# Loading V tiles through GpSimd's DMA queue and K tiles and weights through SyncE's, in a decode kernel with a long key/value cache

## The chip, the cores and the metric

The kernel runs on one core of one Trainium2 chip, the other cores idle. The metric is the device time of one execution in microseconds (us), as the median of several executions. The profile's own span is about 2 us shorter than the device time (383.9 against 385.8 us for the kernel before).

## The reference, cut to what matters

One token is decoded through two branches, mixed by a sigmoid gate. Almost all of the work is the attention branch: 32 query heads share 4 key/value heads ("groups"), and the cache is 65,536 tokens long.

```python
B, Sq, D = (1, 1, 1024)
Hq, Hkv, Sk, Dh = (32, 4, 65536, 128)
...
q = (x @ wq)                                  # reshaped to 32 heads
scores = einsum('bhqd,bhkd->bhqk', q, k) * Dh ** (-0.5)
p = softmax(scores, axis=-1)
o = einsum('bhqk,bhkd->bhqd', p, v)           # k, v: each of 4 heads serves 8 query heads
a = o.reshape(B, Sq, Hq * Dh) @ wo
...                                           # b: a gated MLP with layer norm
return g * a + (1 - g) * b
```

K and V are 67.1 MB each in bfloat16, the weights another 27.8 MB. Each byte is used once, so this is a kernel of loads.

## The kernel before

Each group's K is read as four tiles of 4.19 MB (128 partitions of 32 KB), its V likewise. All large tiles rotate through one pool of four buffers, and one queue, SyncE's, issues every large load in program order:

```python
NKV = 4
kv = ctx.enter_context(tc.tile_pool(name="kv", bufs=NKV))
...
def load(src, shape, name):
    t = kv.tile([P, CT * P], BF16, name=name, tag="kv")
    ...                                        # v: a view of t in the wanted shape
    nc.sync.dma_start(out=v, in_=src)
    return v
```

The main loop works on K of group g beside V of group g-1, because V needs the softmax of the whole group:

```python
for g in range(G):
    for j in range(NT):                        # G = 4 groups, NT = 4 tiles
        k_tile(g, j, load_kv(A_k_cache, g, j, "kn"))
        if j == 1 and g + 1 < G:
            build_w(g + 1)
        if j == NT - 1:
            stats(g)                           # maximum, exp, transposes of the weights
        if g > 0:
            v_tile(g - 1, j, load_kv(A_v_cache, g - 1, j, "vt"))
        elif j == NT - 1:
            project(load(B_w_out..., "wout_t"), ...)
    if g > 0:
        head_out(g - 1)                        # evacuates V's sums, on DVE and PE
for j in range(NT):
    v_tile(G - 1, j, load_kv(A_v_cache, G - 1, j, "vt"))
head_out(G - 1)
...                                            # six loads of wo, 8.4 MB, and the last projection
```

`k_tile` transposes a K tile on DVE in four pieces (`kt`, line 320). When the fourth is done, the tile's buffer is free, and the K tile after the next may be loaded into it. `v_tile` multiplies on PE (line 372) and frees V's buffer. Since K and V loads alternate in program order, K holds two of the four buffers and V the other two.

The point to keep in mind is the order on DVE when a group ends: the maximum over the group, the transposed weights (`stats`), then `head_out(g-1)`, which needs PE to have finished group g-1's last V tile, and only then the transposes of the next group's first K tile.

Of the kernel before, what the change touches and what calls it, by code (L numbers as in the profile page):

```python
# [15 lines left out]
CT = 128  # L16
# [11 lines left out]
def kernel(  # L28
# [15 lines left out]
    nc = tc.nc  # L44

    _, _, D = A_x.shape
    _, G, S, DH = A_k_cache.shape
# [32 lines left out]
    def same_weights(ins):  # L80
        held.add(ins.ins.name)
# [14 lines left out]

    nc.at_finalize(drop_repeated_loads)

    def load(src, shape, name):
        t = kv.tile([P, CT * P], BF16, name=name, tag="kv")  # L100
        n = 1
        for s in shape:
            n *= s
        v = t[:, :n]
        if len(shape) == 2:
            v = v.rearrange("p (a b) -> p a b", b=shape[1])
        nc.sync.dma_start(out=v, in_=src)
        return v

    def load_kv(src, g, j, name):  # L110
        k0 = j * CT * P
        return load(src[0, g, k0:k0 + CT * P, :].rearrange("(p c) d -> p (c d)", c=CT),
                    (CT * DH,), name)


    xg8 = const.tile([KC, 2, P], BF16, name="xg8")
# [6 lines left out]
    KH = KC // 2  # L123
    win_view = B_w_in.rearrange("(p c) n -> p c n", c=KC)
    win_t = [load(win_view[:, i * KH:(i + 1) * KH, :], (KH, F), "win_t") for i in range(2)]
    wq_view = A_wq.rearrange("(p c) n -> p c n", c=KC)
    wq_t = [load(wq_view[:, i * KH:(i + 1) * KH, :], (KH, HD), "wq_t") for i in range(2)]


# [42 lines left out]
    for t in range(2):  # L172
        nc.vector.tensor_tensor(
            out=xm[:, t], in0=xb_ps[:, t * P:(t + 1) * P].rearrange("p (i c) -> p c i", c=KC),
# [51 lines left out]
    for hf in range(2):  # L226
        nc.vector.tensor_tensor(  # L227
            out=zm[:, hf], in0=z_ps[:, hf * HN:hf * HN + ZN].rearrange("p (j c) -> p j c", c=FC),
# [3 lines left out]
                            in_=zm.rearrange("p h j c -> p h c j"), axis=AX.X, op=ALU.add)  # L232
# [44 lines left out]
    for k in range(NHB):  # L277
        xs = slice(k * NX // NHB, (k + 1) * NX // NHB)
        nc.vector.tensor_tensor(  # L279
            out=qm[:, xs], in0=q_ps[:, k * HN:(k + 1) * HN].rearrange("p (x j e) -> p x j e",  # L280
                                                                   j=B, e=2),
# [6 lines left out]
        out=q4[:], in0=q1[:].rearrange("p x e -> p (x e)").unsqueeze(1).to_broadcast(  # L288
            [P, NB, NX * 2]),
# [7 lines left out]
    for g in range(G):  # L297
        k, t0 = g * T2 // NB, g * T2 % NB
        nc.vector.tensor_copy(out=qs[:, g].rearrange("p b (t h) -> p b t h", t=T2),
                              in_=qv[:, k, t0:t0 + T2].rearrange("p t h b -> p b t h"))  # L300

    def build_w(g):
        for v in range(VC):
            nc.vector.tensor_tensor(
                out=wt[g % 2][:, v, :, :, v, :],
                in0=qs[:, g].unsqueeze(2).to_broadcast([P, BP, NB, REP]),
                in1=own_n[:].unsqueeze(1).unsqueeze(3).to_broadcast([P, BP, NB, REP]),
                op=ALU.mult)
# [5 lines left out]
    def k_tile(g, j, kn):  # L314
        kb = kn.bitcast(I32)
        n = CC * DH // 2
        s_ps = pss.tile([P, 2 * HN], FP32, name="s_ps", tag="s")
        for v in range(VC):
            kt = ktp.tile([P, CC * DH], BF16, name="kt")
            nc.vector.transpose(out=kt[:].bitcast(I32), in_=kb[:, v * n:(v + 1) * n])  # L320
            while late:
                nc.vector.reduce_max(**late.pop())  # L322
            kx = kt[:].rearrange("p (c h k e) -> p h e c k", h=2, k=B, e=2)
            for b in range(BP):
                for k in range(2):
                    ins = nc.tensor.matmul(  # L326
                        s_ps[:, k * HN:(k + 1) * HN],
                        lhsT=wt[g % 2][:, v, b].rearrange("p a v h -> p (a v h)"),
                        rhs=kx[:, b // 2, b % 2, k * CC // 2:(k + 1) * CC // 2, :],
                        start=(v == 0 and b == 0), stop=(v == VC - 1 and b == BP - 1),  # L330
                        skip_group_check=True)
                    if k > 0:
                        same_weights(ins)
        if j == 0:
            mxs[g] = wk.tile([P, NT], FP32, name="mx")
        sct[g, j] = scp.tile([P, CC * B], BF16, name="sc")
        nc.scalar.copy(out=sct[g, j][:], in_=s_ps[:])  # L337
        late.append(dict(out=mxs[g][:, j:j + 1], in_=sct[g, j][:], axis=AX.X))

    def stats(g):  # L340
        nc.vector.reduce_max(**late.pop())  # L341
        m1 = wk.tile([P, 1], FP32, name="m1")
        nc.vector.reduce_max(out=m1[:], in_=mxs[g][:], axis=AX.X)  # L343
        mt_ps = psm.tile([1, P], FP32, name="mt_ps", tag="m")
        nc.tensor.transpose(mt_ps[:], m1[:], ident_f[:])  # L345
        gm = wk.tile([1, REP], FP32, name="gm")
        nc.vector.tensor_reduce(out=gm[:], in_=mt_ps[:].rearrange("p (a h) -> p h a", h=REP),
                                axis=AX.X, op=ALU.max)
        gr = wk.tile([1, P // REP, REP], FP32, name="gr")
        nc.vector.tensor_copy(out=gr[:], in_=gm[:].unsqueeze(1).to_broadcast([1, P // REP, REP]))  # L350
        nb_ps = psm.tile([P, 1], FP32, name="nb_ps", tag="m")
        nc.tensor.matmul(nb_ps[:], lhsT=gr[:].rearrange("p a h -> p (a h)"),  # L352
                         rhs=ones_f[0:1, 0:1], start=True, stop=True)
        nb = wk.tile([P, 1], FP32, name="nb")
        nc.vector.tensor_scalar(out=nb[:], in0=nb_ps[:], scalar1=-SCALE, scalar2=None,  # L355
                                op0=ALU.mult)
        lss[g] = wk.tile([P, NT], FP32, name="ls")
        for j in range(NT):
            nc.scalar.activation(out=sct[g, j][:], in_=sct[g, j][:], func=ACT.Exp, scale=SCALE,  # L359
                                 bias=nb[:, 0:1], accum_out=lss[g][:, j:j + 1])  # L360
            ptt[g, j] = ptp.tile([P, CC, B], BF16, name="pt")
            nc.vector.transpose(out=ptt[g, j][:].rearrange("p c x -> p (c x)"),  # L362
                                in_=sct[g, j][:])

    def v_tile(g, j, vt):
        if j == 0:
            o_ps[g] = pso.tile([P, 2, VC * DH], FP32, name="o_ps")
        vx = vt.rearrange("p (v c d) -> p c v d", v=VC, d=DH)
        for u in range(CC // 2):
            hs = slice(u % 2 * P // 2, (u % 2 + 1) * P // 2)  # L370
            for e in range(2):
                ins = nc.tensor.matmul(  # L372
                    o_ps[g][hs, e, :],
                    lhsT=ptt[g, j][:, 2 * u:2 * u + 2, :].rearrange("p c x -> p (c x)"),
                    rhs=vx[:, 2 * u + e], start=(j == 0 and u < 2),
                    stop=(j == NT - 1 and u >= CC // 2 - 2), skip_group_check=True)
                if e > 0:
                    same_weights(ins)
# [32 lines left out]
    def project(w, n, vec, c0, first=False, last=False):  # L411
        for c in range(n):
            for t in range(NB):
                nc.tensor.matmul(  # L414
                    out_ps[t * B:(t + 1) * B, :],
                    lhsT=vec[:, c0 + c:c0 + c + 1].to_broadcast([P, B]),
                    rhs=w[:, c, t * NO:(t + 1) * NO],
                    start=(first and c == 0), stop=(last and c == n - 1),
                    skip_group_check=True)
# [3 lines left out]
# [5 lines that stand above are left out]
            if j == NT - 1:  # L428
                stats(g)
            if g > 0:  # L430
                v_tile(g - 1, j, load_kv(A_v_cache, g - 1, j, "vt"))
            elif j == NT - 1:
                project(load(B_w_out.rearrange("(p c) n -> p c n", c=FC), (FC, D), "wout_t"),
                        FC, uT, 0, first=True)
        if g > 0:
            head_out(g - 1)
    for j in range(NT):
        v_tile(G - 1, j, load_kv(A_v_cache, G - 1, j, "vt"))
    head_out(G - 1)


# [52 lines left out]
```

## Time and profile before

| what | value | view |
|---|---|---|
| time | 385.78 us (385.75 to 385.80) | runs |
| SyncE's queue | 162.01 MB, 98.5% of 16 engines | DMA queues |
| rate in mid-kernel | 430 to 431 GB/s | windows |
| PE, DVE busy | 63%, 57% | busy table |
| from the landing of a group's last K tile to the release of the next group's first | 36 us | timelines |

From the page of the kernel before: the span; the busy engines; the share of DMA engines' time in 40 slices (9 is 90% or more) and the rate in each; the queues; the chain that ended last.

```profile
span 383.9 us, 2650 instructions
PE 242.3 (63%) x1372; PEld 59.3 (15%) x796; DVE 218.5 (57%) x211; ACT 39.6 (10%) x55; POOL 4.4 (1%) x10
DMA  8999999999999999999999999999999999999995
GB/s 335 430 437 437 435 434 430 423 431 426 428 427 437 435 430 437 427 434 430 423 432 427 437 437 422 430 434 437 427 425 427 437 438 427 425 430 431 434 411 203
q1 hardware_dynamic: 6192, 162.01, 98.5%
DMA 60%; DVE 20%; PE 11%; issue 5%; ACT 2%; SPq 1%; DVEq 0%; ACTq 0%
kn<-in_A_k_cache_dram SPq DMA_DIRECT2D x16, 4096.0 KB, 26.5
vt<-in_A_v_cache_dram SPq DMA_DIRECT2D x16, 4096.0 KB, 32.9
```

One queue keeps all 16 engines busy but for the first and the last few microseconds; compute is used to two thirds. The last number of the two load lines is the time from issue to landing. A tile takes 9.73 us to move, so a K load lands after waiting for about two others: there is always something queued. Windows of the same kernel (for each stretch: its length, the busy time of the engines, then granted clock, DMA share and GB/s):

```profile
95.00:173.00 78.00, 53.16 (x296) 13.18 (x178) 48.37 (x37) 10.99 (x14) 0.00 (x0) 0.81 1.00 431
173.00:251.00 78.00, 54.48 (x265) 11.94 (x135) 50.33 (x40) 8.69 (x12) 0.00 (x0) 0.81 1.00 430
251.00:329.00 78.00, 54.36 (x267) 11.98 (x137) 49.93 (x36) 8.91 (x13) 0.00 (x0) 0.81 1.00 431
```

A share of 1.00 in every 78 us (eight tiles of 9.73 us each: four of one group's K, four of the V before it) and a rate of 430 to 431 GB/s say that no load was issued too late. The timeline of DVE at the end of group 1, counted from 0 (start, duration, instruction; in brackets how long DVE was idle before it and what ended that):

```profile
156.71 2.31 DVE L320 STREAM_TRANSPOSE kt<-kn 128x2048 int32<-128x2048 int32 x1 [9.43 <-DMA kn<-in_A_k_cache_dram]
160.04 6.68 DVE L320 STREAM_TRANSPOSE kt<-kn 128x2048 int32<-128x2048 int32 x3
183.97 8.87 DVE L320 STREAM_TRANSPOSE kt<-kn 128x2048 int32<-128x2048 int32 x4
195.60 2.31 DVE L320 STREAM_TRANSPOSE kt<-kn 128x2048 int32<-128x2048 int32 x1 [2.77 <-DMA kn<-in_A_k_cache_dram]
```

Group 1's last K tile lands at 156.7 us. DVE comes to the next group's first tile only at 184.0, 27 us later, and has freed it at 192.9. In these 36 us only one K buffer, that of the last tile itself, is given back (at 166.7), where in mid-group one comes back about every 19 us. DVE still waits for data afterwards (2.77 us at 195.6), so the stream, not DVE, sets the pace.

### The profile page before, as it was taken

What the parts mean: (1) busy time and instruction counts of PE and PEld (TensorE: products, weight loads), DVE (VectorE), ACT (ScalarE), POOL (GpSimd) and SP (SyncE); (2) the same over time, 40 slices, a digit from 0 to 9 for tenths busy, and PEclk for the clock granted to TensorE, in tenths of its full rate; (3) what the DMA queues carried; (4) which work ended last, traced back from release to release, by engine and by line L of the source; (5) the groups of instructions that cost most, each with busy time, mean ns of one, the idle gap of its engine ahead of it and who ended that gap; (6) DMA issues with size and microseconds to landing.
All of it is one profiled execution on the core that took longest, in us unless ns stands there. A gap on an engine that the chain in (4) does not pass through costs nothing.

```text
span 383.9 us, 2650 instructions
## 1 busy us (share of the span) xinstructions
PE 242.3 (63%) x1372; PEld 59.3 (15%) x796; DVE 218.5 (57%) x211; ACT 39.6 (10%) x55; POOL 4.4 (1%) x10
## 2 busy tenths in 40 slices
PE   0433447976449948466699393774993937685553
PEld 0110001111202201011121020121220201121122
DVE  5141478988497563658975545679754546730040
ACT  1010001100511101014011010140110101400000
POOL 4000000000000000000000000000000000000000
PEclk9996559889659989686599797865997869888868
DMA  8999999999999999999999999999999999999995
GB/s 335 430 437 437 435 434 430 423 431 426 428 427 437 435 430 437 427 434 430 423 432 427 437 437 422 430 434 437 427 425 427 437 438 427 425 430 431 434 411 203
DMA packets 6248, 162.18 MB, mean 422 GB/s; under 512 B 728, under 2 KB 732, under 8 KB 1116
## 3 DMA queue, kind: packets, MB, share of 16 engines
q1 hardware_dynamic: 6192, 162.01, 98.5%
q8 instruction: 8, 0.13, 0.1%
q14 instruction: 4, 0.03, 0.0%
q10 hardware_dynamic: 44, 0.01, 0.0%
HBM read 162.01 MB, written 0.00 MB: 422 GB/s over the span
## 4 chain that ended last, share of the span: by engine, by line
DMA 60%; DVE 20%; PE 11%; issue 5%; ACT 2%; SPq 1%; DVEq 0%; ACTq 0%
DMA kn<-in_A_k_cache_dram 47%; DVE kt L320 16%; DMA wo_t<-in_A_wo_dram 8%; PE s_ps L326 8%; DMA win_t<-in_B_w_in_dram 5%; DVE pt L362 2%; PE o_ps L372 2%; ACT sc L337 1%; PE z_ps L213 1%; ACT sc L359 1%; DVE mx L341 1%; DVE o_sb L387 0%; SPq L449 0%; ACT L359 0%; PE nb_ps L352 0%
## 5 line engine op out<-in xcount | busy, mean ns | idle before, releaser
L326 PE MATMUL s_ps<-kt,wt 128*128 128x512 bf16 x512 | 142.3, 437 | 67.9 <-DVE kt L320 67.3
L320 DVE STREAM_TRANSPOSE kt<-kn 128x2048 int32<-128x2048 int32 x64 | 143.3, 2284 | 63.5 <-DMA kn<-in_A_k_cache_dram 63.4
L372 PE MATMUL o_ps<-vt,pt 128*64 128x512 bf16 x512 | 69.2, 432 | 8.8 <-DMA vt<-in_A_v_cache_dram 8.8
L326 PEld LDWEIGHTS <-wt 128*128 128x128 bf16 x256 | 27.6, 108 | 184.0 <-issue 122.9
L337 ACT CAST sc<-s_ps 128x1024 bf16<-128x1024 f32 x16 | 16.2, 1013 | 253.8 <-PE s_ps L326 253.8
L372 PEld LDWEIGHTS <-pt 128*64 128x64 bf16 x256 | 17.2, 124 | 57.9 <-issue 56.4
L362 DVE STREAM_TRANSPOSE pt<-sc 128x1024 bf16<-128x1024 bf16 x16 | 18.6, 1218 | 6.8 <-ACT sc L359 6.8
L383 DVE TENSOR_TENSOR om<-o_ps,own 128x1024 f32<-128x1024 f32 x4 | 4.8, 1205 | 26.8 <-PE o_ps L372 26.8
L359 ACT ACTIVATE sc<-sc,nb 128x1024 bf16<-128x1024 bf16 x16 | 18.2, 1139 | 10.2 <-DVE nb L355 10.2
L322 DVE TENSOR_REDUCE mx<-sc 128x1 f32<-128x1024 bf16 x12 | 14.3, 1192 | 4.4 <-ACT sc L337 4.4
L341 DVE TENSOR_REDUCE mx<-sc 128x1 f32<-128x1024 bf16 x4 | 4.9, 1220 | 12.3 <-ACT sc L337 12.3
L213 PE MATMUL q_ps<-wq_t,xT 128*32 128x512 bf16 x64 | 7.2, 630 | 7.3 <-DMA wq_t<-in_A_wq_dram 7.3
L393 PE MATMUL om_ps<-o_sb,hsel 128*32 128x128 f32 x8 | 2.4, 398 | 13.6 <-DVE o_sb L387 13.6
L213 PE MATMUL z_ps<-win_t,xT 128*32 128x448 bf16 x64 | 6.4, 577 | 4.9 <-DMA win_t<-in_B_w_in_dram 4.9
L414 PE MATMUL out_ps<-wo_t,oa 128*32 128x256 bf16 x128 | 6.3, 346 | 4.6 <-DMA wo_t<-in_A_wo_dram 3.2
L279 DVE TENSOR_TENSOR rowt<-q_ps,own_b 128x512 f32<-128x512 f32 x2 | 1.3, 686 | 12.4 <-PE q_ps L213 12.4
L345 PE MATMUL mt_ps<-ident_f,m 128*1 128x128 f32 x4 | 1.4, 346 | 10.2 <-DVE m L343 10.2
L387 DVE TENSOR_REDUCE o_sb<-om 128x128 f32<-128x1024 f32 x4 | 7.5, 1871 | 0.1
L227 DVE TENSOR_TENSOR rowt<-z_ps,own_b 128x448 f32<-128x448 f32 x2 | 1.2, 620 | 9.6 <-PE z_ps L213 9.6
L213 PEld LDWEIGHTS <-xT 128*32 128x32 bf16 x64 | 3.0, 140 | 20.3 <-issue 20.3
L453 ACT CAST out_sb<-out_ps 128x256 bf16<-128x256 f32 x1 | 0.4, 372 | 47.6 <-PE out_ps L414 47.6
L414 PEld LDWEIGHTS <-oa 128*32 128x32 bf16 x128 | 4.2, 119 | 6.9 <-issue 4.2
(88 smaller groups left out, 57.9 us busy)
## 6 DMA issues: line engine op xcount, KB each, us to landing
kn<-in_A_k_cache_dram SPq DMA_DIRECT2D x16, 4096.0 KB, 26.5
vt<-in_A_v_cache_dram SPq DMA_DIRECT2D x16, 4096.0 KB, 32.9
wq_t<-in_A_wq_dram SPq DMA_DIRECT2D x2, 4096.0 KB, 28.4
win_t<-in_B_w_in_dram SPq DMA_DIRECT2D x2, 3584.0 KB, 15.1
wo_t<-in_A_wo_dram SPq DMA_DIRECT2D x1, 4096.0 KB, 27.2
wout_t<-in_B_w_out_dram SPq DMA_DIRECT2D x1, 3584.0 KB
wo_t<-in_A_wo_dram SPq DMA_DIRECT2D x1, 2048.0 KB
wo_t<-in_A_wo_dram SPq DMA_DIRECT2D x1, 1024.0 KB
```

Of the source, the lines that this page charges most:

```text
L213: ins = nc.tensor.matmul(ps[t * B:(t + 1) * B, k * HN:k * HN + n], lhsT=xT[:, i * KH + c:i * KH + c + 1].to_broadcast([P, B]), rhs=w[:, c, ...
L320: nc.vector.transpose(out=kt[:].bitcast(I32), in_=kb[:, v * n:(v + 1) * n])
L322: nc.vector.reduce_max(**late.pop())
L326: ins = nc.tensor.matmul(s_ps[:, k * HN:(k + 1) * HN], lhsT=wt[g % 2][:, v, b].rearrange("p a v h -> p (a v h)"), rhs=kx[:, b // 2, b % 2, ...
L337: nc.scalar.copy(out=sct[g, j][:], in_=s_ps[:])
L341: nc.vector.reduce_max(**late.pop())
L359: nc.scalar.activation(out=sct[g, j][:], in_=sct[g, j][:], func=ACT.Exp, scale=SCALE, bias=nb[:, 0:1], accum_out=lss[g][:, j:j + 1])
L362: nc.vector.transpose(out=ptt[g, j][:].rearrange("p c x -> p (c x)"), in_=sct[g, j][:])
L372: ins = nc.tensor.matmul(o_ps[g][hs, e, :], lhsT=ptt[g, j][:, 2 * u:2 * u + 2, :].rearrange("p c x -> p (c x)"), rhs=vx[:, 2 * u + e], sta ...
L383: nc.vector.tensor_tensor(out=om8[:], in0=o_ps[g][:].rearrange("p e (v d) -> p (e v) d", d=DH), in1=own_8[:].unsqueeze(2).to_broadcast([P, ...
L387: nc.vector.tensor_reduce(out=o_sb[:], in_=om8[:].rearrange("p x d -> p d x"), axis=AX.X, op=ALU.add)
L414: nc.tensor.matmul(out_ps[t * B:(t + 1) * B, :], lhsT=vec[:, c0 + c:c0 + c + 1].to_broadcast([P, B]), rhs=w[:, c, t * NO:(t + 1) * NO], st ...
```

## The change

The intent: each DMA engine then has two rings with work, one from each queue, and V loads need not be issued in line with K loads. (A ring is the line of packets that one queue has waiting at one DMA engine.)

```diff
-    def load(src, shape, name):
+    def load(src, shape, name, queue=None):
 ...
-        nc.sync.dma_start(out=v, in_=src)
+        (queue or nc.sync).dma_start(out=v, in_=src)
 ...
             if g > 0:
-                v_tile(g - 1, j, load_kv(A_v_cache, g - 1, j, "vt"))
+                v_tile(g - 1, j, load_kv(A_v_cache, g - 1, j, "vt", nc.gpsimd))
 ...
     for j in range(NT):
-        v_tile(G - 1, j, load_kv(A_v_cache, G - 1, j, "vt"))
+        v_tile(G - 1, j, load_kv(A_v_cache, G - 1, j, "vt", nc.gpsimd if j % 2 == 0 else None))
```

(`load_kv` hands `queue` on.) Of 16 V loads 14 go through GpSimd's queue; the last group's second and fourth stay on SyncE's. Buffers and compute instructions are the same.

More of the change, by code (lines that the diff above doesn't have):

```diff
@@ L106, in load, with load_kv @@
             v = v.rearrange("p (a b) -> p a b", b=shape[1])
-        nc.sync.dma_start(out=v, in_=src)
+        (queue or nc.sync).dma_start(out=v, in_=src)
         return v
-    def load_kv(src, g, j, name):
+    def load_kv(src, g, j, name, queue=None):
         k0 = j * CT * P
         return load(src[0, g, k0:k0 + CT * P, :].rearrange("(p c) d -> p (c d)", c=CT),
-                    (CT * DH,), name)
+                    (CT * DH,), name, queue)
     xg8 = const.tile([KC, 2, P], BF16, name="xg8")
```

## The prediction

> **What bounds the kernel now.** The DMA engines. The DMA page shows one queue (SyncE's) carrying 162.01 MB and filling 98.5% of the 16 engines' span. The windows view gives share 1.00 and 430 to 431 GB/s in each of 95:173, 173:251 and 251:329 us. K tile 6 is picked up at 117.8 us, the last at 312.4: 20 tiles of 4.19 MB, 9.73 us each. PE is busy 63%, DVE 57%; DVE's longest wait is for K loads (63.4 us), and the chain of waits is 60% DMA. Outside the stream lie about 2 us before the first bytes and 3.3 us after the last.
>
> **What the change does.** It removes no byte. 14 of the 16 V loads (36% of the bytes) go to GpSimd's queue. SyncE's issue costs 0.33 us per tile (timeline) and comes with about two tiles queued ahead (V lands 32.9 us after its issue), so the issue time saved is hidden. SyncE's in-order waits (159 us for transposes, 50 us for the V matmuls) no longer hold one stream for the other, but every buffer is released by the same instruction as before, and the load stream has no hole to fill.
>
> The Trainium skill, "DMA: Bandwidth & Descriptors", section "Issuing engines are not separate DMA queues", says that all issuers share the same 16 engines; "Queues, rings and completion order" says that each engine takes turns between rings, packet by packet. This trace has one busy ring, so it can show neither.
>
> **Gain.** A second ring can only fill gaps between packets. The page's best slices reach 437 to 438 GB/s against 431: at most 1.5%, or 4 us over the 260 us in which both rings carry loads; I expect 0 to 1.
>
> **Loss.** Turns change the order of landing: a K tile and its V tile, now 9.7 us apart, travel and land together, K up to 6 to 10 us later than now. Mid-group there is slack: a K buffer is released 10 us after landing, V's about 16, against 19.4 us for a pair. A group's end is tight: from the pick-up of its last K tile (156.7) to the load that the next group's first K tile releases (192.9) pass 36 us. Now 48 us of loads are queued or issued in between; with K and V landing together about 39. So I expect no hole, or one of 1 to 2 us, at each of two group changes. GpSimd's descriptor writing may delay V loads, hidden while SyncE's ring has work. In the tail the last two V tiles land closer together, but 19.4 us of output weights follow and hide it. A cost I can't size from this trace: if some engines run slower on GpSimd's descriptors, 36% of the bytes carry that.
>
> **Predicted: 386.5 us** (before 385.78), range 382 to 394. Faster by over 2%: 0.04; within 2%: 0.85; slower by over 2%: 0.11.
>
> **What would show each step.** (1) Two queues of about 103 and 59 MB, shares summing to about 98%. (2) 429 to 435 GB/s between 95 and 329 us. (3) K's time to landing some us over 26.5; V's shorter or equal. (4) DVE's waits for K the same in sum within 10 us; perhaps a slice under 425 GB/s after a group's end (near 190 to 205 and 268 to 283 us). (5) The end unchanged: output weights land last, about 31 us of the chain.
>
> **What would make it wrong.** Slower: GpSimd's descriptors smaller or slower per packet, engines that finish unevenly, or holes of several us at group changes. Faster: two rings overlapping each other's per-packet cost, so that the stream runs at 438 GB/s or above.

## The result, and the profile after

| | before | after |
|---|---|---|
| median of the runs | 385.79 us (n = 4) | 386.84 us (386.58 to 387.13, n = 4) |
| ratio, 95% interval | | 1.0027 [1.0013, 1.0041] |
| span of the profiled run | 383.9 us | 384.8 us |

Ratios here are the mean time of one kernel's runs over that of the other's of the same rounds, so not quite the ratio of the medians quoted. The change costs 1.05 us, clear of noise and far under 2%. The profiled run is the fastest of the four (386.58 us), so the profile can place about 0.9 us of it.

From the page after:

```profile
span 384.8 us, 2660 instructions
PE 239.2 (62%) x1372; PEld 59.1 (15%) x796; DVE 218.7 (57%) x211; ACT 39.6 (10%) x55; POOL 11.9 (3%) x24
DMA  8999999999999999999999999999999999999994
GB/s 334 429 436 436 434 433 436 429 433 429 417 429 429 433 431 436 436 436 429 429 433 393 436 436 434 427 436 426 433 433 421 433 433 433 433 428 429 429 413 185
q1 hardware_dynamic: 4176, 103.29, 62.8%
q0 software_dynamic: 2016, 58.72, 35.5%
DMA 56%; DVE 20%; PE 16%; issue 5%; ACT 2%; SPq 1%; ACTq 0%; DVEq 0%
kn<-in_A_k_cache_dram SPq DMA_DIRECT2D x16, 4096.0 KB, 30.2
vt<-in_A_v_cache_dram POOLq DMA_DIRECT2D x14, 4096.0 KB, 27.4
```

Two queues now share the bytes, and their shares add up to 98.3% where one had 98.5%. K loads land 3.7 us later after their issue, V loads 5.5 us earlier. One slice sticks out: 393 GB/s, the 22nd, from 202 to 212 us. A slice counts a packet where it starts, so single slices are rough. The windows place the loss in the same stretch:

```profile
95.00:173.00 78.00, 48.25 (x268) 11.64 (x162) 44.25 (x32) 9.97 (x13) 2.12 (x4) 0.78 1.00 430
173.00:251.00 78.00, 57.57 (x283) 12.89 (x144) 53.12 (x41) 9.70 (x13) 2.11 (x4) 0.84 1.00 427
251.00:329.00 78.00, 54.21 (x261) 12.22 (x135) 49.36 (x35) 7.67 (x11) 2.64 (x5) 0.78 1.00 431
```

427 against 430 GB/s over 78 us is 0.5 us of lost streaming. The share is 1.00 even here: the ten 32 KB packets that SyncE's ring started between 202.8 and 203.3 us took 1.5 to 2.2 us, where the median is 1.216 (trace). The bytes moved since the start say it most exactly (MB, counted from the packet records of the two traces, each packet spread over the time that it took):

```
          95 us   155 us   203 us   205 us   320 us
before    39.90    65.73    86.42    87.28   136.81
after     39.88    65.72    86.40    87.04   136.60
```

Two rings carry loads from about 87 us on, and up to 203 us not a tenth of a us is lost. Within the next 2 us the stream falls 0.24 MB behind, 0.55 us at 431 GB/s, and after that nothing more. The timeline of DVE shows the group's end that goes with it:

```profile
165.13 2.31 DVE L320 STREAM_TRANSPOSE kt<-kn 128x2048 int32<-128x2048 int32 x1 [9.42 <-DMA kn<-in_A_k_cache_dram]
168.46 6.69 DVE L320 STREAM_TRANSPOSE kt<-kn 128x2048 int32<-128x2048 int32 x3
192.97 11.06 DVE L320 STREAM_TRANSPOSE kt<-kn 128x2048 int32<-128x2048 int32 x5
```

Group 1's last K tile lands 8.4 us later than before (165.1 against 156.7), and everything of the group's end moves with it. At 193.0 DVE does five transposes in a row without a wait: the next K tile had landed while DVE was still busy. Both K buffers were taken, so no K load could be issued until the first of the two tiles was transposed. That load went out 9 us later than in the kernel before (timelines of SyncE, first before, then after):

```profile
192.86 0.33 SPq L107 DMA_DIRECT2D kn<-in_A_k_cache_dram  x1
201.87 0.33 SPq L107 DMA_DIRECT2D kn<-in_A_k_cache_dram  x1
```

From 197.5 us on only the V load on GpSimd's ring had packets left, it ran out from about 203 us on, and the new load finished its first packet at 204.5.

The end of the two timelines gives the rest of the difference. Before, the last projection and the output:

```profile
380.69 0.29 PE L414 MATMUL out_ps<-wo_t,oa 128*32 128x256 bf16 x4 [0.36 <-DMA wo_t<-in_A_wo_dram]
381.43 0.61 ACTq L454 DMA_DIRECT2D out_dram<-out_sb  x1
```

After:

```profile
381.13 0.29 PE L414 MATMUL out_ps<-wo_t,oa 128*32 128x256 bf16 x4 [0.35 <-DMA wo_t<-in_A_wo_dram]
381.87 0.61 ACTq L454 DMA_DIRECT2D out_dram<-out_sb  x1
```

In both, PE waits for the last piece of output weights, so the stream still sets the end; it lands 0.44 us later. From the issue of the output to the end of the span pass 2.47 us before (383.9 - 381.43) and 2.93 after (384.8 - 381.87): another 0.46 us. The two terms sum to 0.9 us, the difference of the spans.

### The profile page after: what moved, and what is told of

Its sections match the earlier page's. It is cut to its first block, busy times and chain, and to the rows that moved or that the text cites. A ratio compares the mean times of both kernels' runs of the same rounds, so it can differ in the third digit from the quotient of the medians.

```text
span 384.8 us, 2660 instructions
## 1 busy us (share of the span) xinstructions
PE 239.2 (62%) x1372; PEld 59.1 (15%) x796; DVE 218.7 (57%) x211; ACT 39.6 (10%) x55; POOL 11.9 (3%) x24
## 3 DMA queue, kind: packets, MB, share of 16 engines
q1 hardware_dynamic: 4176, 103.29, 62.8%
q0 software_dynamic: 2016, 58.72, 35.5%
## 4 chain that ended last, share of the span: by engine, by line
DMA 56%; DVE 20%; PE 16%; issue 5%; ACT 2%; SPq 1%; ACTq 0%; DVEq 0%
DMA kn<-in_A_k_cache_dram 47%; DVE kt L320 15%; PE s_ps L326 10%; DMA wo_t<-in_A_wo_dram 6%; PE o_ps L372 4%; DMA wb<-in_B_b_sp_dram 2%; ACT sc L337 1%; DVE pt L362 1%; SPq L449 1%; DVE o_sb L387 1%; PE z_ps L213 1%; DVE mx L341 1%; DVE om L383 1%; ACT sc L359 0%; PE om_ps L393 0%
## 5 line engine op out<-in xcount | busy, mean ns | idle before, releaser
L320 DVE STREAM_TRANSPOSE kt<-kn 128x2048 int32<-128x2048 int32 x64 | 143.3, 2283 | 68.4 <-DMA kn<-in_A_k_cache_dram 67.5
L372 PE MATMUL o_ps<-vt,pt 128*64 128x512 bf16 x512 | 68.2, 428 | 12.1 <-DMA vt<-in_A_v_cache_dram 11.9
L107 POOL DMA_DIRECT2D vt<-in_A_v_cache_dram x14 | 7.5, 539 | 316.0 <-PE o_ps L372 135.5
```

The costliest lines, as they stand in the source:

```text
L107: (queue or nc.sync).dma_start(out=v, in_=src)
L320: nc.vector.transpose(out=kt[:].bitcast(I32), in_=kb[:, v * n:(v + 1) * n])
L372: ins = nc.tensor.matmul(o_ps[g][hs, e, :], lhsT=ptt[g, j][:, 2 * u:2 * u + 2, :].rearrange("p c x -> p (c x)"), rhs=vx[:, 2 * u + e], sta ...
```

## The experiments

Two theories of the 1.05 us were set against each other, and a third beside them. (A descriptor is the note that tells a DMA engine what to move; the profile calls GpSimd's queue `software_dynamic` and SyncE's `hardware_dynamic`.)

- **A**: engines take turns between rings, so K and V land together; at the first group change the engines run dry once (about 0.5 us). The end of the program costs about 0.45 us more when GpSimd's queue was used. Descriptors written by GpSimd are as good as any.
- **R1**: GpSimd's descriptors slow the stream in proportion to the bytes that they carry.
- **R2**: an engine loses time whenever it turns from one ring to the other.

All ten kernels gave correct results. Times and ratios against the kernel before, from the same rounds:

| kernel | median us | ratio | 95% interval |
|---|---|---|---|
| one_v | 386.01 | 1.0005 | 0.9992 to 1.0017 |
| early_k | 386.20 | 1.0011 | 0.9999 to 1.0024 |
| all_pool | 397.02 | 1.0296 | 1.0279 to 1.0313 |
| act_v | 386.30 | 1.0014 | 1.0001 to 1.0028 |
| before_delay | 385.80 | 1.0001 | 0.9984 to 1.0017 |
| after_delay | 390.39 | 1.0123 | 1.0108 to 1.0138 |
| wo_pool | 393.41 | 1.0203 | 1.0180 to 1.0225 |
| late_pool | 385.99 | 1.0006 | 0.9992 to 1.0019 |
| act_v_delay | 391.03 | 1.0138 | 1.0124 to 1.0152 |
| four_v | 386.47 | 1.0017 | 0.9999 to 1.0035 |

### wo_pool: do the engines take turns?

From the kernel before, one line:

```diff
-            nc.sync.dma_start(out=t[:, c0 - b:c0 - b + n, :], in_=wo_view[:, c0:c0 + n, :])
+            nc.gpsimd.dma_start(out=t[:, c0 - b:c0 - b + n, :], in_=wo_view[:, c0:c0 + n, :])
```

> Before, with only the six output-weight loads (8.4 MB) on GpSimd's queue. At about 343 us, when they are issued, 17.6 us of V loads are still waiting on SyncE's ring. If each engine takes turns between its rings packet by packet, the weights take half the engines from then on, the last V tile lands near 378 us and not 361, and the end follows 5.3 us of V matmuls, 5.3 us of head sums and 5.7 us of projection later: span about 397 us, time about 399 us. If the engines serve the older loads first, whichever ring they come by, nothing moves: 386.2 us.

Measured: 393.41 us, 7.6 us slower. The V matmuls of the last two tiles in wo_pool (timeline of PE):

```profile
353.79 5.80 PE L372 MATMUL o_ps<-vt,pt 128*64 128x512 bf16 x32 [4.98 <-DMA vt<-in_A_v_cache_dram]
372.04 5.22 PE L372 MATMUL o_ps<-vt,pt 128*64 128x512 bf16 x32 [12.44 <-DMA vt<-in_A_v_cache_dram]
```

and in the kernel before:

```profile
351.25 5.33 PE L372 MATMUL o_ps<-vt,pt 128*64 128x512 bf16 x32 [4.42 <-DMA vt<-in_A_v_cache_dram]
360.96 5.33 PE L372 MATMUL o_ps<-vt,pt 128*64 128x512 bf16 x32 [4.38 <-DMA vt<-in_A_v_cache_dram]
```

The last V tile lands 11 us later, because weights that were issued after it, on the other ring, take every other turn. Counting the trace's records of finished 32 KB packets shows the turns (columns: stretch of 2 us, placed to about 1 us; packets of GpSimd's ring; of SyncE's):

```
352  13  11
354  12  14
356  15  15
358  10  12
360  15  12
362  15  14
```

Half and half. The direction was as expected, the size was not: 17 us of delay and 399 us were expected, 11 and 393 came, since the weights were issued at 345.7 and not 343.4 us, their first packets finished only at about 350, and by then less of V was left. "Older loads first" is out.

### all_pool: a control that failed, and why

K, V and all output weights through GpSimd's queue; the first four weight loads stay on SyncE's.

```diff
-        k_tile(g, j, load_kv(A_k_cache, g, j, "kn"))
+        k_tile(g, j, load_kv(A_k_cache, g, j, "kn", nc.gpsimd))
 ...                                           # likewise V, wout and wo
```

> All K, V and output weights through GpSimd's queue in the program order of before; only the first four weight loads stay on SyncE's. One ring at a time, so the order of landing is that of before, but 91% of the bytes have GpSimd's descriptors. A: no dry stretch, only the end's 0.45 us: 386.2 us. R1: the loss grows with the bytes, about 2.5 us: 388.3 us. R2: no turning, no loss: 385.8 to 386.2 us.

Measured: 397.02 us, 11.2 us slower, and neither figure. The page of all_pool:

```profile
GB/s 328 451 438 428 424 424 429 412 325 374 368 325 413 328 428 449 434 434 428 424 426 424 444 441 429 425 428 424 432 431 443 431 422 431 433 428 431 434 411 174
```

All of the loss lies between about 75 and 140 us; from 155 to 345 us the windows give 430 GB/s in both kernels. It comes from the handing over between the queues: the first K loads, on their own ring, took turns with the query weights that had been issued before them. The second half of those weights reached PE at 59.4 us where it had been 39.8 (timeline of PE, line 213), and the first K transpose came at 67.5 us where it had been 50.7. By then K tiles had taken all four buffers, and further loads had to wait for DVE: they went out at 76.7, 88.7, 100.3 and 111.9 us, 11.5 to 12.1 us apart where a tile takes 9.73, and the engines ran dry in between. The run says nothing against GpSimd's descriptors, and it was repeated with the handing over moved.

### late_pool: the control mended

As all_pool, but everything up to group 0 stays on SyncE's queue; K from group 1 on, all V and wo go through GpSimd's.

```diff
+        k_tile(g, j, load_kv(A_k_cache, g, j, "kn", nc.gpsimd if g > 0 else None))
 ...                                           # likewise all of V and wo
```

> The control that all_pool failed to be: everything up to group 0 stays on SyncE's queue (weights, the first four K tiles, the first output weights), and from group 1 on all K, V and output weights go through GpSimd's queue in the program order of before. The two rings overlap only for a few us at the handing over, near 72 to 95 us; after that one software ring, with 78% of the bytes. A (landing order and a cost at the end, descriptors free): no dry stretch, last V tile about 9.7 us after the one before it as in before, out issue to end of span 2.9 us and not 2.5, 386.2 to 386.5 us. R1 (GpSimd's descriptors slow the stream in proportion to bytes): 388 us or more.

Measured: 385.99 us, ratio 1.0006: the same as before, a little under what was expected. GpSimd's queue carried 76.3% of the engines' span:

```profile
q0 software_dynamic: 4768, 125.83, 76.3%
q1 hardware_dynamic: 1296, 36.18, 22.1%
```

Twice the bytes of the change on GpSimd's queue, and no loss of the stream (87.26 MB at 205 us, 136.78 at 320, a constant 0.02 to 0.03 MB from the kernel before): R1 is out. The trace's records of single packets say it too. A 32 KB packet (one partition's row) took, as median and 5th to 95th percentile:

```
before      SyncE's queue     4480 packets  1.216 us  1.213 to 1.224
after       SyncE's queue     2688 packets  1.216 us  1.213 to 1.224
after       GpSimd's queue    1792 packets  1.216 us  1.213 to 1.224
late_pool   GpSimd's queue    3712 packets  1.216 us  1.214 to 1.224
act_v       ScalarE's queue   1792 packets  1.216 us  1.214 to 1.224
```

Sixteen engines times 32,768 bytes over 1.216 us is 431.2 GB/s: the rate of the mid-kernel windows before. There was no gap between packets for a second ring to fill, and turning between rings adds none: the table of bytes above has no loss in the 116 us with two rings before 203 us, nor after 205, so R2 is out too. The slices of 437 GB/s on the page are no faster stretches; with each packet spread over the time that it took, the kernel before has 428 to 431 GB/s in every slice from 48 to 374 us.

### early_k: take away the late release

From the kernel after: `head_out(g-2)` moves behind the first K tile of the group, so DVE transposes that tile first and its buffer is free earlier.

```diff
             if j == NT - 1:
                 stats(g)
+            if j == 0 and g > 1:
+                head_out(g - 2)
             if g > 0:
                 v_tile(...)
 ...
-        if g > 0:
+        if g == G - 1:
             head_out(g - 1)
```

> After, with the sum of the heads of group g-1 moved behind the first K tile of the next group, so that this K tile's buffer is released about 5 to 7 us earlier. A: the dry stretch near 200 us goes, every slice of the stream is at 427 GB/s or more, the last weight piece lands at about 380.7 us of the span as before, time about 386.3 us (0.5 less than after, 0.5 more than before). R1 and R2: nothing of what they name is touched, 386.8 us.

Measured: 386.20 us, as expected; all five runs lie below all four of the kernel after (386.12 to 386.43 against 386.58 to 387.13), but the intervals of this ratio and of the change's own overlap, so the trace has to carry the argument. Timeline of DVE in early_k:

```profile
186.09 8.85 DVE L320 STREAM_TRANSPOSE kt<-kn 128x2048 int32<-128x2048 int32 x4
201.54 2.31 DVE L320 STREAM_TRANSPOSE kt<-kn 128x2048 int32<-128x2048 int32 x1 [1.83 <-DMA kn<-in_A_k_cache_dram]
```

The tile is transposed 7 us earlier (186.1 against 193.0) and DVE is again the one to wait. The last output-weight piece reaches PE at 380.73 us, before 380.69, after 381.13: the 0.44 us are gone. So is the dry stretch: 87.28 MB at 205 us and 136.81 at 320, to the digit as before, with two rings and GpSimd's descriptors as in the kernel after. Output issue to end is 2.93 us as in the kernel after, so only the term at the end is left. One point of the expectation missed: four slices in mid-stream are under 427 GB/s (407, 419 and twice 426). The kernel before has slices of 422 and 423 too; slices were a poor criterion, and where the stream ends is a good one.

### act_v: two hardware rings

From the kernel after: V on ScalarE's queue. Since the kernel keeps each engine's instructions in program order, each V load is issued one step ahead, just before a cast that waits for later work of PE, and buffers are chosen by hand so that each load uses the same one as before.

```diff
+        n = g * NT + j - (NT - 1)
+        if 0 <= n:
+            load_v(n, nc.scalar)               # V tile n, used in the next step
+        if n == 12:
+            load_v(14, nc.scalar)
         nc.scalar.copy(out=sct[g, j][:], in_=s_ps[:])
 ...
-                v_tile(g - 1, j, load_kv(A_v_cache, g - 1, j, "vt", nc.gpsimd))
+                v_tile(g - 1, j, vts.pop((g - 1) * NT + j))
```

> After, with the 14 V loads on ScalarE's hardware queue in place of GpSimd's, each issued just ahead of a cast that waits for later work of PE anyway, so at nearly the same moments; the buffer of every load is the same one. Two hardware rings. A: K and V still land together and the engines still run dry once near 200 us, but the end costs nothing extra: about 386.3 us. R1: no software descriptors, 385.8 us. R2: turning as before, 386.8 us.

Measured: 386.30 us, the number expected; where it comes from is not shown. The profiled run was the fastest of the five (385.87; the others 386.25 to 386.50), and it does not show a dry stretch: the load that the next group's first K tile releases was issued at 200.88 us, and the K tile on its way landed at about 201.9, 1 us later. In the kernel after that load went out at 201.87, and the stream ran dry. In both, the load's first packets start at about 202.8 us; they take the usual 1.2 us in act_v and up to 2.2 us in the kernel after. One microsecond decides. That the four slower runs of act_v went dry is likely but not shown. Its end, output issue to end of span, took 2.51 us, as without GpSimd.

### before_delay, after_delay, act_v_delay: make the late release later

Four extra reductions on DVE, 4.6 us together, at the end of the first two `head_out`, in the kernel before, in the one after and in act_v:

```diff
+        if g < 2:
+            junk = wk.tile([P, 4], FP32, name="junk")
+            for i in range(4):
+                nc.vector.reduce_max(out=junk[:, i:i + 1],
+                                     in_=om8[:].rearrange("p x d -> p (x d)"), axis=AX.X)
```

> Before, with four extra reductions (1.2 us each, 4.8 us together) on DVE at the end of the sum of heads 0 and 1, which holds back the first K transposes of the next group. With one ring about 48 us of loads are queued when the group's last K tile is picked up, and the release takes 36: the slack is about 12 us. Theory A: no loss, 385.8 us within 0.3. Rival (the group changes are not where anything is lost, or the two kernels are equally near to running dry): same loss as in after with the same reductions.

> After, with the same four extra reductions. With K and V landing together the engines already run dry at the first group change, so A expects the whole 4.8 us there and 0 to 4 us at the second (which had a few us of slack): 391.5 to 395.5 us, with a slice far under 425 GB/s near 200 to 210 us. Rival: no more loss than before with the same reductions.

> act_v (V on ScalarE's hardware queue) with the four extra reductions of before_delay and after_delay. If the lost slack belongs to K and V landing together and not to GpSimd: a dry stretch after the first group change as in after_delay, 389 to 390.3 us, of which nothing at the end (out issue to end of span 2.5 us). If it belongs to GpSimd's queue: 385.8 to 386.5 us.

Measured: 385.80, 390.39 and 391.03 us. One ring hides all of the delay; with two rings most or all of it is paid, whichever engine issues the second: 3.6 us more than the kernel after, 4.7 us more than act_v. Windows of the three kernels around the first and the second group change (columns as above). First before_delay:

```profile
190.00:200.00 10.00, 8.87 (x32) 1.78 (x16) 9.85 (x5) 0.00 (x0) 0.00 (x0) 0.74 1.01 431
200.00:210.00 10.00, 9.93 (x62) 2.35 (x31) 8.60 (x8) 1.01 (x1) 0.00 (x0) 1.00 0.98 423
276.00:286.00 10.00, 10.00 (x62) 2.35 (x31) 7.89 (x5) 1.01 (x1) 0.00 (x0) 1.00 0.98 423
```

The same windows of after_delay:

```profile
190.00:200.00 10.00, 1.43 (x5) 0.39 (x4) 9.40 (x12) 0.00 (x0) 0.00 (x0) 0.56 0.98 423
200.00:210.00 10.00, 10.00 (x41) 1.98 (x20) 7.81 (x4) 1.00 (x1) 0.00 (x0) 0.76 0.72 277
276.00:286.00 10.00, 9.86 (x42) 2.08 (x22) 8.86 (x5) 0.85 (x1) 0.00 (x0) 0.80 0.99 426
```

And of act_v_delay:

```profile
190.00:200.00 10.00, 0.64 (x2) 0.18 (x2) 9.15 (x11) 0.00 (x0) 0.00 (x0) 0.55 1.01 433
200.00:210.00 10.00, 9.37 (x36) 1.98 (x20) 9.35 (x5) 0.23 (x1) 0.00 (x0) 0.76 0.48 175
276.00:286.00 10.00, 9.77 (x42) 2.08 (x22) 8.95 (x5) 0.87 (x1) 0.00 (x0) 0.81 0.98 423
```

The DMA share between 200 and 210 us falls from 0.98 to 0.72 and 0.48. (423 - 277) / 431 of 10 us is 3.4 us, (423 - 175) / 431 is 5.8; bytes counted as above put after_delay 3.9 us and act_v_delay 5.5 us behind at 212 us, and no further behind up to 340. So at the second group change, 276 to 286 us, nothing is lost in any of them. after_delay stayed 1 us under its expected range, act_v_delay 0.7 us over its own; why ScalarE's kernel runs dry longer was not followed up (its K transposes there start 1.7 us later, at 198.3 against 196.6 us).

### one_v and four_v: the end of the program

The kernel before with one, and with four, V loads on GpSimd's queue:

```diff
-                v_tile(g - 1, j, load_kv(A_v_cache, g - 1, j, "vt"))
+                v_tile(g - 1, j, load_kv(A_v_cache, g - 1, j, "vt",
+                                         nc.gpsimd if (g, j) == (1, 0) else None))   # four_v: if g == 1
```

> Before, with only the very first V load on GpSimd's queue. Theory A (the 1.05 us that the change costs are two terms: about 0.5 us of dry DMA engines at the first group change, caused by the order of landing, and about 0.45 us at the very end of the program that any use of GpSimd's queue costs): about 0.45 us over before, 386.2 us, all of it between the issue of the output and the end of the span; no slow slice near 200 us. Rival R1 (GpSimd's descriptors slow the load stream in proportion to the bytes they carry): 1/14 of the loss, under 0.1 us. Rival R2 (an engine loses time when it turns between two rings): under 0.1 us too.

> Before, with the four V loads of group 0 on GpSimd's queue, to see what the end of the program costs: out issue to end of span was 2.47 us in before, 2.58 with one load on that queue, 2.93 with 14, 2.97 with 38. If the cost goes with the number of completion semaphores in use by that queue[...], four loads give about 2.7 us; if it goes with the number of loads, 2.6 us; if it is there in full from a few loads on, 2.9 us.

Measured: 386.01 us for one_v, +0.17 and not +0.45; 386.47 us for four_v (two runs). From output issue to end of span, one profile of each kernel:

| kernel | loads on GpSimd's queue | output issue to end, us |
|---|---|---|
| before, before_delay, act_v, act_v_delay | 0 | 2.47, 2.52, 2.51, 2.53 |
| one_v | 1 | 2.58 |
| late_pool | 34 | 2.68 |
| after, after_delay, early_k | 14 | 2.93, 2.89, 2.93 |
| all_pool | 39 | 2.97 |
| four_v | 4 | 3.27 |
| wo_pool | 6 | 3.43 |

The spans are rounded to 0.1 us, so each figure is good to 0.05; with the spans unrounded (trace) the four kernels without that queue have 2.49 to 2.51 us and the eight with it 2.63 to 3.42. All kernels that use GpSimd's queue thus take longer at the end than all that do not, by about 0.1 to 0.9 us. The cost does not grow with the number of loads, and none of the rules offered in the expectation fits four_v. What it depends on stays open.

## Why the prediction was right

The predicted time was 386.5 us, the measured one 386.84, and the class "within 2%" was right. Step by step:

1. **"It removes no byte ... the load stream has no hole to fill": right.** Shares of 62.8% and 35.5% against 98.5%; 430, 427 and 431 GB/s in the three windows against 431, 430 and 431.
2. **Shared engines and turns, taken from the Trainium skill, "DMA: Bandwidth & Descriptors", sections "Issuing engines are not separate DMA queues" and "Queues, rings and completion order": agreed.** Packets take 1.216 us on every queue, and in wo_pool the two rings finish packets half and half.
3. **The gain: "at most 1.5%, or 4 us ... I expect 0 to 1": right in the end, but the bound was read wrongly.** The 437 GB/s slices were taken for a reachable rate. Back-to-back packets of 1.216 us make 431.2 GB/s, which the kernel before already had (430 to 431); the bound was close to zero.
4. **The loss: "I expect no hole, or one of 1 to 2 us, at each of two group changes": one hole, at the first change alone, 0.5 us.** The mechanism was right: K 8.4 us later at the group's end, and 36.7 us from the landing of its last tile to the load that the next group's first tile releases (165.13 to 201.87), against about 39 us of loads. By these two figures alone there would have been no hole; what the sum left out is the start of a load: issued at 201.87, it finished its first packet at 204.53, 1.4 us more than a packet's own 1.2. The delayed kernels show the lost slack: 4.6 us of delay are free with one ring and cost 3.6 and 4.7 us with two. The second change had slack that was not foreseen; after_delay loses nothing there.
5. **"The end unchanged": half right.** The last two V tiles were multiplied in one go at 361.4 us and the output weights hid it, as said; but their part of the chain was 25 us (24.8 in one piece), not 31, and the end took 0.46 us longer after the output had been issued, as it took longer in every kernel with GpSimd's queue. The prediction had no such term. That the number still came within 0.4 us is in part luck: the missing term made up for a hole smaller than the middle of its range.
6. **"If some engines run slower on GpSimd's descriptors": not seen.** late_pool lands its tiles as the kernel before does.

So the intended gain went nowhere: a second ring can only add work to engines that lack it, and these had none of their time left over.

## What to carry to other kernels

When the packets on the DMA engines follow each other without a gap (here 1.216 us each, 431 GB/s), another queue cannot add rate; it changes who gets the next turn. A load on a second ring takes every other turn from loads issued earlier on the first one, so put loads that are needed first on the same ring and ahead of the others, or keep one ring in the order of use (moving the wrong loads cost 7.6 and 11.2 us here). And judge a change of order by the slack at the place where buffers come back latest: this one costs 1 us of time but used up the slack at the first group change, which had hidden 4.6 us of extra work on DVE; more work on DVE there would now be paid for.

## What the Trainium skill lacked or had wrong

- "DMA: Bandwidth & Descriptors", section "Rules for kernel authors", says that spreading DMAs over issuing engines for bandwidth does not help. The runs agree (1.216 us for a packet on all three queues) but add that it can hurt: turns delay earlier loads of the other ring, by 11 us for the last V tile in wo_pool and by 19.6 us for the query weights in all_pool.
- The same page, section "SWDGE vs HWDGE vs iDMA", gives 4096 B as the preferred bound of a packet. The records of these traces show 32,768 B in one packet, from SyncE's, ScalarE's and GpSimd's queues alike. A packet takes its 1.216 us whether or not the other ring has work, so the turns are of that size too.
- The same page, section "Where 436 GB/s comes from", gives a ceiling of 435.2 GB/s. Engines that never pause reached 431.2 here (16 x 32,768 bytes in 1.216 us).
- No page that was read has a cost at the end of a program for having used GpSimd's queue: about 0.1 to 0.9 us in eight kernels (one profile of each), by a rule that is not known.
